# Converting the second network's weights in two of eight units, with partial results in the attention's PSUM banks

## The chip, the core and the metric

The kernel runs on one core of a Trainium2 chip. The metric is the device time of one launch in microseconds. The core has five engines with queues of their own: TensorE (PE) for matrix products, VectorE (DVE), ScalarE (ACT), GpSimd (POOL), and SyncE (SP), which issues the DMAs here. The engines wait for each other by semaphores. Each of them works its instructions off in the order in which the built program has them.

## The reference

Three stages follow each other: a gated linear attention over 768 time steps for 4 batches and 8 heads, a first network whose activation is a rational function, and a second one with a SoLU activation and a layer norm.

```python
for t in range(S):
    state = alpha[:, :, t, :, None] * state + np.einsum('bhd,bhe->bhde', k[:, :, t], v[:, :, t])
    y[:, :, t] = np.einsum('bhd,bhde->bhe', q[:, :, t], state)
...
h = x @ w_in
P = a[0] + a[1] * h + a[2] * h2 + a[3] * h3
Q = 1.0 + np.abs(b[0]) * np.abs(h) + np.abs(b[1]) * h2
g = P / (Q + 1e-06)
return (g @ w_out).astype(np.float32)
...
h = x @ w_in
sm = e / (np.sum(e, axis=-1, keepdims=True) + 1e-09)
solu = h * sm
ln = (solu - mu) / np.sqrt(var + 1e-06) * g_ln
return (ln @ w_out).astype(np.float32)
```

There are 3072 tokens of width 384; the first network is 2048 wide, the second 1024. The weights arrive as 64-bit floating-point numbers, so that they must be converted on the chip.

## The kernel before

The 768 steps are cut into 6 chunks of 128, and the first network works on one chunk (512 tokens over the batches) at a time, in 16 **units** of 128 columns of its hidden layer. So there are 96 units, numbered u from 0 to 95, in the loop at line 873. A unit multiplies up into a PSUM tile `hp` (line 590, 9 matmuls; every product is made of three, with values split into a high and a low part), evaluates the rational function on ACT, DVE and POOL (lines 595 to 624; on DVE the lines 616, 619, 620 and 621, and `fin[u]` is the last of them), and four units later multiplies down into `x2p` (line 636, 9 matmuls). `hp` has three PSUM banks, so the products of unit u + 3 wait for `fin[u]`.

The attention runs beside this, half a chunk in 8 units: six of the eight units have an attention step (`take(side, 1)`, line 900, begun anew where u modulo 8 is 2). The steps of PE are scores (`sc`, line 420), outputs (`y`, line 444) and state updates (`u`, line 483). All of them use one PSUM pool of two banks, the tag `at`. DVE reads `y` in line 471 and `u` in line 493. The steps of DVE prepare the next half chunk (lines 302 to 334: transposes, two scans, products).

The weights of the second network are converted in the same loop, by `w2_split`: 14 pieces, 6 of 128x512 and 8 of 128x384 numbers. A piece is loaded into a tile `st` (line 531), three integer operations on DVE put together a 32-bit number (lines 535, 538 and 539), ACT scales it (line 544, the last 8 pieces only) and makes the high part (545), POOL the low part (546), and a DMA writes both to DRAM (line 548). `st` has two buffers, which `x2e` (line 644, at the end of each chunk) uses too. The stage ends before u = 80, where the weights are read back.

Before the loop the weights of the first network go through the same `split_w`, with `stage["bank"]` at `"x2"`. There the result of lines 535 and 538, `fp`, lies in PSUM; from u = 0 on the bank is `""`, and `fp` is the SBUF tile `ft` itself.

The program is put in order by a scheduler that works from the order of the code and from dependencies. `later(n)` (line 839) adds one: what is issued in it stands behind `fin[u - n]`. `order` rows below show what comes of it.

Of the kernel before, what the change touches and what calls it, by code (L numbers as in the profile page):

```python
# [7 lines left out]
F32 = mybir.dt.float32  # L8
# [15 lines left out]
def _run(*gens):  # L24
    for g in gens:
        for _ in g:
            pass
# [3 lines left out]
def kernel(  # L31
# [23 lines left out]
    NTOK = B * CH  # L55
    KT = DM // 128
    NF1 = DF1 // 128
# [23 lines left out]
    SKIP = (5, 7, 11)  # L81
    AHEAD = 3
    LATE = 2
    U2, TP = 16, 0.3
    assert (B, H, D, CH) == (4, 8, 48, 128)

    const = ctx.enter_context(tc.tile_pool(name="const", bufs=1, side="left"))
# [55 lines left out]
    def judge(moe_pool):  # L143

        sums = const.tile([128, 1], F32, name="sums")
        row = moe_pool.tile([1, 128], F32, name="row", tag="ft", bufs=2)
        tot = const.tile([1, 1], F32, name="tot")
        nc.vector.tensor_reduce(sums, bad, axis=AX.X, op=ALU.add)
        nc.sync.dma_start(out=row, in_=sums)
        nc.vector.tensor_reduce(tot, row, axis=AX.X, op=ALU.add)  # L150
        nc.vector.tensor_scalar(flag, tot, 0.0, None, ALU.is_gt)

    def network(fast):
# [6 lines left out]
        ps_hp = ps_h.__enter__()  # L160
        if fast:
# [3 lines left out]
            ps_ap = ps_a.__enter__()  # L165
# [26 lines left out]
        def borrow(n, o, dims):  # L192
            if n not in lent:
                lent[n] = moe_pool.tile([128, GW], F32, name=f"lent{n}", tag=f"g{n}")
            size = 1
            for d in dims:
                size *= d
            t = lent[n][:, o:o + size]
            if len(dims) == 1:
                return t  # L200
            nm = "abcd"[:len(dims)]
            return t.rearrange(f"p ({' '.join(nm)}) -> p {' '.join(nm)}", **dict(zip(nm, dims)))
# [302 lines left out]
        stage = {"n": 0, "wide": False, "bank": None}  # L505

        def split_w(src, hi, lo, scale=None):
            keep = None
            if hi is None:
                keep, raw = lo, moe_pool.tile([128, NTOK], I64, name="st", tag="st", bufs=2)  # L510
                n = src.shape[1]
                both = raw[:].bitcast(F32R)
                hi, lo = both[:, :n], both[:, n:2 * n]
            n = src.shape[1]
            x = stage["n"]
            stage["n"] += 1
            ft = moe_pool.tile([128, NTOK], F32, name="ft", tag="ft", bufs=2)
            if stage["bank"] == "x2":
                fp = ps_x2p.tile([128, NTOK], F32, name="fp", tag=f"x2p{x % KT}")
            elif stage["bank"] == "h":  # L520
                fp = ps_hp.tile([128, NTOK], F32, name="fp", tag="h")
            else:
                fp = ft
            if src.dtype == I64:
                if keep is not None:
                    st = raw
                elif stage["wide"] and x % 6 not in (0, 2):
                    st = borrow(2, 2048 + 1024 * (0, 0, 0, 1, 2, 3)[x % 6], [2 * NTOK]).bitcast(I64)
                else:
                    st = moe_pool.tile([128, NTOK], I64, name="st", tag="st", bufs=2)  # L530
                nc.sync.dma_start(out=st[:, :n], in_=src)
                w32 = st[:, :n].bitcast(I32).rearrange("p (n t) -> p n t", t=2)
                fi = ft[:, :n].bitcast(I32)
                gi = fp[:, :n].bitcast(I32)
                nc.vector.tensor_scalar(  # L535
                    gi, w32[:, :, 1], 3, 0x3FFFFFF8, ALU.logical_shift_left, ALU.bitwise_and
                )
                nc.vector.scalar_tensor_tensor(gi, w32[:, :, 1], -0x40000000, gi, ALU.bitwise_and, ALU.bitwise_or)  # L538
                nc.vector.scalar_tensor_tensor(fi, w32[:, :, 0], 29, gi, ALU.logical_shift_right, ALU.bitwise_or)  # L539
            else:  # L540
                nc.sync.dma_start(out=ft[:, :n], in_=src)
            f = ft[:, :n]
            if scale is not None:
                nc.scalar.activation(f, f, AF.Copy, scale=scale)
            nc.scalar.activation(hi, f, AF.Copy)
            nc.gpsimd.tensor_tensor(lo, f, hi.bitcast(F32), ALU.subtract)
            if keep is not None:
                nc.sync.dma_start(out=keep, in_=both[:, :2 * n].bitcast(F32).rearrange("p (x n) -> p x n", x=2))
# [102 lines left out]
        def w2_split():  # L651
            nc.sync.dma_start(out=gln, in_=moe2_g_ln.rearrange("(f p) -> p f", p=128))
            for o in range(0, DF2, 512):
                for kt in range(KT):
                    split_w(moe2_w_in[128 * kt:128 * kt + 128, o:o + 512], None, w2i_d[:, :, kt, o:o + 512])
                    yield
            for f in range(NF2):
                split_w(moe2_w_out[128 * f:128 * f + 128, :], None, w2o_d[:, :, f, :], scale=gln[:, f:f + 1])
                yield

        def w2_load(nm):
            src = {"i": w2i_d, "o": w2o_d}[nm]
            n, step = {"i": (KT, 1), "o": (NF2, 4)}[nm]
            for z in range(0, n, step):
                for x, y in enumerate("hl"):
                    nc.sync.dma_start(out=w2[nm + y][:, z:z + step].bitcast(F32), in_=src[:, x, z:z + step])
                    yield
# [126 lines left out]
        def take(g, n):  # L794
            for _ in range(n):
                if next(g, "end") == "end":
                    return False
            return True

        def chain(*gens):  # L800
            for g in gens:
                yield from g
# [47 lines left out]
        def half_steps(i):  # L850
            gp = a_pe(i)
            gd = chain(a_prep(i + 1), a_move_qk(i + 1) if i + 1 >= NPE else iter(()), a_load(i + 2, ("ra", "rk")) if i + 2 < NH and i + 1 >= NPE else iter(())) if i + 1 < NH else iter(())
            while True:
                with pin(GP):
                    a = next(gp, "end")
                with pin(GS):
                    b = next(gd, "end")
                    if b != "end":
                        b = next(gd, "end")
                if a == "end" and b == "end":  # L860
                    if i + 1 < NH:
                        _run(a_enter(i + 1))
                        if i + 2 < NH and i + 1 < NPE:
                            _run(a_load(i + 2))
                    return
                yield

        split2 = w2_split() if fast else iter(())
        tp = 0.0
        side = iter(())  # L870
        tail = None
        prep = iter(())
        for u in range(NU + LAG):
            c, f = divmod(u, NF1)
            now[0] = u
            if f % (NF1 // 2) == LATE and u < NU:
                _run(side)
                i = 2 * c + 2 + f // (NF1 // 2)
                side = half_steps(i) if fast and i < NH else iter(())
            if u < NU:  # L880
                if f == 0 and c == NCH - 1:
                    if fast:
                        judge(moe_pool)
                    open2()
                    tail = chain(w2_load("i"), n_load(0), w2_load("o"))
                if f == 0 and c and not fast:
                    x_load(c)
                if fast and u < NF1:
                    if f % 4 == 0:
                        _run(prep)  # L890
                        prep = w1_group(f // 4 + 2) if f < 8 else iter(())
                    with later(G1):
                        take(prep, 1)
                m_up(u)
                if fast and u < NF1:
                    with later(G1):
                        take(prep, 1)
            if u == NU:
                _run(n_load(1))
            take(side, 1)  # L900
            if u >= U2:
                tp += TP
                with later(G2):
                    take(split2, int(tp))
                tp -= int(tp)
            if tail is not None:
                _run(split2)
                take(tail, 2)
            if u >= LAG:
                m_down(u - LAG)  # L910
            if u - NU + NF1 in EARLY:
                n_tile(EARLY.index(u - NU + NF1))
                if len(EARLY) == B and u - NU + NF1 == EARLY[-1]:
                    n_turn(0)
# [108 lines left out]
    with tc.If(wide > 0):  # L1023
        recurrence()
        network(False)
# [30 lines left out]
```

## Time and profile before

| | |
|---|---|
| median of 3 runs | 798.67 us (797.55 to 798.87) |
| the profiled execution | 796.42 us |
| its span, first to last instruction | 794.7 us |
| PE busy | 732.0 us, 92% of the span |
| DVE busy | 643.2 us, 81% |
| ACT busy | 535.5 us, 67% |
| POOL busy | 359.5 us, 45% |

The span is what the trace covers; 1.7 us of the execution's own time lie around it. Busy shares are means over stages. The unit loop runs to about 600 us of the span; what follows is the second network alone. A unit is recognized in the trace by its one ACT instruction of line 623, which makes the high part of its result.

### The profile page before, as it was taken

The page shows a single profiled execution, that of the slowest core. Times are in us where ns is not written, and L with a number is a line of the kernel's source. Part 1 is how long each engine was busy: PE and PEld are TensorE (multiplying, and loading weights), DVE is VectorE, ACT ScalarE, POOL GpSimd, SP SyncE. Part 2 cuts the span into 40 slices and gives each one's busy share as a digit, 9 for nine tenths or more (in the row PEclk, how much of TensorE's full clock was granted, in tenths as well). Part 3 has the DMA queues.
Part 4 walks back from the last instruction along what each step waited for, and adds up shares of the span by engine and source line. Part 5 has one row for each costly group of instructions (what it writes and reads, how often), then busy time and mean ns, then how long its engine had stood idle before and what let it go on. Part 6 is the DMA issues. An engine that isn't in the chain of part 4 may idle for free.

```text
span 794.7 us, 13903 instructions
## 1 busy us (share of the span) xinstructions
PE 732.0 (92%) x4976; PEld 606.9 (76%) x4976; DVE 643.2 (81%) x1110; ACT 535.5 (67%) x983; POOL 359.5 (45%) x306
## 2 busy tenths in 40 slices
PE   4864986999999989999999999999999999999996
PEld 3753765787777877687777788888888989998996
DVE  5999999979799998979897976567877698777630
ACT  2335756787787868788878879788775555455541
POOL 3256776856555344545454334243242524352322
PEclk9767898999999999999999999999999999999998
DMA  7956466365837275445826160460014443542552
GB/s 172 268 165 187 126 185 134 98 129 164 208 94 179 94 210 143 134 106 162 197 81 160 64 122 15 144 255 0 1 42 106 138 107 100 145 97 60 137 122 69
DMA packets 87279, 101.75 MB, mean 128 GB/s; under 512 B 34464, under 2 KB 63136, under 8 KB 87200
## 3 DMA queue, kind: packets, MB, share of 16 engines
q1 hardware_dynamic: 87104, 100.67, 48.0%
q8 instruction: 41, 0.67, 0.4%
q14 instruction: 38, 0.31, 0.1%
q10 hardware_dynamic: 96, 0.10, 0.0%
HBM read 60.59 MB, written 27.56 MB: 111 GB/s over the span
## 4 chain that ended last, share of the span: by engine, by line
PE 45%; DVE 27%; ACT 7%; DMA 7%; issue 7%; POOL 3%; SPq 3%; DVEq 0%; POOLq 0%; ACTq 0%
PE h L710 13%; PE op L774 12%; PE x2p L636 10%; PE hp L590 9%; DVE ft L539 2%; POOL gl L624 2%; SPq L266 2%; DVE p L616 2%; DVE w L619 2%; DVE alT L324 2%; DVE ft L538 2%; DVE qk L290 2%; DVE p L621 2%; DVE hp L620 2%; DVE ft L535 1%
## 5 line engine op out<-in xcount | busy, mean ns | idle before, releaser
L590 PE MATMUL hp<-xt,g 128*128 128x512 f32 x864 | 226.2, 404 | 16.7 <-DVE p L621 7.7
L590 PEld LDWEIGHTS hp<-xt,g 128*128 128x128 f32 x864 | 163.7, 193 | 59.5 <-DVE p L621 14.2
L624 POOL TENSOR_TENSOR gl<-p,gh 128x512 fp32r<-128x512 f32 x96 | 129.1, 1344 | 175.1 <-ACT gh L623 101.4
L636 PE MATMUL x2p<-gh,g 128*128 128x512 f32 x576 | 196.0, 395 | 0.6 <-ACT gh L623 0.6
L636 PEld LDWEIGHTS x2p<-gh,g 128*128 128x128 f32 x576 | 108.3, 189 | 26.3 <-ACT gh L623 1.4
L636 PE MATMUL x2p<-gl,g 128*128 128x512 f32 x288 | 113.6, 394 | 1.4 <-POOL gl L624 1.4
L774 PE MATMUL op<-w2oh,room 128*128 128x384 f32 x384 | 101.8, 339 | 0.1
L766 POOL TENSOR_TENSOR room<-room,room 128x1024 fp32r<-128x1024 f32 x22 | 53.6, 2438 | 102.2 <-ACT room L765 98.2
L619 DVE SCALAR_TENSOR_TENSOR w<-w,co,hp 128x512 f32<-128x512 f32 x84 | 61.8, 736 | 42.8 <-ACT hp L618 42.4
L710 PE MATMUL h<-w2ih,x 128*128 128x512 f32 x288 | 90.8, 394 | 0.0
L597 ACT ACTIVATE p<-hp,co 128x512 f32<-128x512 f32 x96 | 65.9, 687 | 13.9 <-POOL gl L624 13.4
L618 ACT ACTIVATE hp<-ah 128x512 f32<-128x512 f32 x84 | 50.1, 597 | 32.9 <-DVE p L616 32.2
L616 DVE SCALAR_TENSOR_TENSOR p<-p,co,hp 128x512 f32<-128x512 f32 x84 | 61.7, 734 | 12.7 <-ACT p L597 12.2
L598 ACT ACTIVATE w<-ah,co 128x512 f32<-128x512 f32 x96 | 69.3, 723 | 3.1 <-DVE hp L620 2.9
L774 PEld LDWEIGHTS op<-w2oh,room 128*128 128x128 f32 x384 | 70.0, 188 | 1.7 <-DVE room L766 0.5
L595 ACT ACTIVATE ah<-hp 128x512 f32<-128x512 f32 x96 | 56.7, 590 | 15.9 <-PE hp L590 15.8
L636 PEld LDWEIGHTS x2p<-gl,g 128*128 128x128 f32 x288 | 54.3, 189 | 14.5 <-POOL gl L624 2.6
L623 ACT ACTIVATE gh<-p 128x512 fp32r<-128x512 f32 x96 | 59.9, 624 | 8.1 <-PE x2p L636 3.0
L774 PE MATMUL op<-w2ol,room 128*128 128x384 f32 x192 | 65.0, 339 | 0.0
L621 DVE SCALAR_TENSOR_TENSOR p<-p,co,hp 128x512 f32<-128x512 f32 x84 | 62.2, 740 | 1.2
L710 PEld LDWEIGHTS h<-w2ih,x 128*128 128x128 f32 x288 | 53.9, 188 | 11.7
L617 ACT ACTIVATE ah<-w,co 128x512 f32<-128x512 f32 x84 | 60.6, 722 | 1.3
(168 smaller groups left out, 1281.1 us busy)
## 6 DMA issues: line engine op xcount, KB each, us to landing
room<-room SPq DMA_DIRECT2D x96, 128.0 KB, 2.3
qk_d<-qk SPq DMA_DIRECT2D x10, 771.0 KB, 4.0
st<-in_moe_w_in_dram SPq DMA_DIRECT2D x15, 512.0 KB, 4.9
st<-in_moe_w_out_dram SPq DMA_DIRECT2D x18, 384.0 KB, 4.2
qks<-qk_d SPq DMA_DIRECT2D x20, 257.0 KB, 5.1
x<-x_d SPq DMA_DIRECT2D x18, 256.0 KB, 3.7
out_dram<-o SPq DMA_DIRECT2D x94, 48.0 KB, 1.6
ra<-in_alpha_dram SPq DMA_DIRECT2D x44, 96.0 KB, 2.5
```

The costliest lines, as they stand in the source:

```text
L590: last["PE", u] = nc.tensor.matmul(hp, lhsT=w[:, kt, 128 * o:128 * o + 128], rhs=xts[c][:, kt, xx, :], start=(kt == 0 and w is hi and xx = ...
L597: nc.scalar.activation(p, hp, AF.Square, bias=co[:, 7:8])
L598: nc.scalar.activation(w, ah, AF.Square, bias=co[:, 6:7])
L616: nc.vector.scalar_tensor_tensor(p, p, a1, hp, ALU.add, ALU.mult)
L617: nc.scalar.activation(ah, w, AF.Ln, bias=rest)
L619: nc.vector.scalar_tensor_tensor(w, w, rest, hp, ALU.add, ALU.mult)
L621: fin[u] = nc.vector.scalar_tensor_tensor(p, p, a0, hp, ALU.add, ALU.mult)
L623: last["ACT", u] = nc.scalar.activation(gh, p, AF.Copy)
L624: last["POOL", u] = nc.gpsimd.tensor_tensor(gl, p, gh[:].bitcast(F32), ALU.subtract)
L636: nc.tensor.matmul(x2ps[c][d], lhsT=w[:, o, 128 * d:128 * d + 128], rhs=gg, start=(f == 0 and w is hi and gg is gh), stop=(f == NF1 - 1 an ...
L710: nc.tensor.matmul(hp[:, 512 * n:512 * n + 512], lhsT=x2s[c][:, kt, x, CH * b:CH * b + CH], rhs=w2[w][:, kt, 512 * n:512 * n + 512], start ...
L774: nc.tensor.matmul(op, lhsT=x[:, 128 * f:128 * f + 128], rhs=w2[w][:, f, :], start=(f == 0 and x is hi and w == "oh"), stop=(f == NF2 - 1 ...
```

## The change

A piece was converted whenever a running sum, which grew by 0.3 in each unit from u = 16 on, passed a whole number: about three pieces in ten units, whatever the attention did in that unit. Now a piece is converted in the units from u = 15 on whose number modulo 8 is 0 or 7, one in each: u = 15, 16, 23, 24, and so on to 64. The integer results `fp` go to a tile of the attention's PSUM pool. `later(G2)` is as before.

```diff
--- before.py
+++ after.py
@@ -81,7 +81,7 @@
     SKIP = (5, 7, 11)
     AHEAD = 3
     LATE = 2
-    U2, TP = 16, 0.3
+    U2, IDLE = NF1 - 1, (0, NF1 // 2 - 1)
     assert (B, H, D, CH) == (4, 8, 48, 128)
 
     const = ctx.enter_context(tc.tile_pool(name="const", bufs=1, side="left"))
@@ -517,8 +517,8 @@
             ft = moe_pool.tile([128, NTOK], F32, name="ft", tag="ft", bufs=2)
             if stage["bank"] == "x2":
                 fp = ps_x2p.tile([128, NTOK], F32, name="fp", tag=f"x2p{x % KT}")
-            elif stage["bank"] == "h":
-                fp = ps_hp.tile([128, NTOK], F32, name="fp", tag="h")
+            elif stage["bank"] == "at":
+                fp = ps_ap.tile([128, NTOK], F32, name="fp", tag="at")
             else:
                 fp = ft
             if src.dtype == I64:
@@ -866,7 +866,6 @@
                 yield
 
         split2 = w2_split() if fast else iter(())
-        tp = 0.0
         side = iter(())
         tail = None
         prep = iter(())
@@ -898,11 +897,10 @@
             if u == NU:
                 _run(n_load(1))
             take(side, 1)
-            if u >= U2:
-                tp += TP
+            if u >= U2 and f % (NF1 // 2) in IDLE:
+                stage["bank"] = "at"
                 with later(G2):
-                    take(split2, int(tp))
-                tp -= int(tp)
+                    take(split2, 1)
             if tail is not None:
                 _run(split2)
                 take(tail, 2)
```

On DVE the pieces now stand together. The rows are those of DVE in the second half of units 36 to 38, as they stand before: three pieces are near, two of them ahead of or between the two reads of `y` (L471).

```order
L535 TENSOR_SCALAR ft<-st 128x512
L619 SCALAR_TENSOR_TENSOR w<-w,co,hp 128x512
L538 SCALAR_TENSOR_TENSOR ft<-st,ft 128x512
L620 SCALAR_TENSOR_TENSOR hp<-w,hp 128x512
L539 SCALAR_TENSOR_TENSOR ft<-st,ft 128x512
L621 SCALAR_TENSOR_TENSOR p<-p,co,hp 128x512
L535 TENSOR_SCALAR ft<-st 128x384
L616 SCALAR_TENSOR_TENSOR p<-p,co,hp 128x512
L538 SCALAR_TENSOR_TENSOR ft<-st,ft 128x384
L471 TENSOR_TENSOR xt<-y,xt 128x2x256
L539 SCALAR_TENSOR_TENSOR ft<-st,ft 128x384
L471 TENSOR_TENSOR xt<-y,xt 128x256
```

After the change the same place, from the reads of `y` on:

```order
L471 TENSOR_TENSOR xt<-y,xt 128x2x256
L471 TENSOR_TENSOR xt<-y,xt 128x256
L620 SCALAR_TENSOR_TENSOR hp<-w,hp 128x512
L535 TENSOR_SCALAR fp<-st 128x384
L621 SCALAR_TENSOR_TENSOR p<-p,co,hp 128x512
L538 SCALAR_TENSOR_TENSOR fp<-st,fp 128x384
L539 SCALAR_TENSOR_TENSOR ft<-st,fp 128x384
L616 SCALAR_TENSOR_TENSOR p<-p,co,hp 128x512
L535 TENSOR_SCALAR fp<-st 128x384
L538 SCALAR_TENSOR_TENSOR fp<-st,fp 128x384
L539 SCALAR_TENSOR_TENSOR ft<-st,fp 128x384
L493 TENSOR_TENSOR Sbd<-Sbd,u 48x8x48 x2
```

The reads of `y` have moved ahead of the pieces, and two pieces stand as a block between them and L493, which frees the bank of `u`. It is so, with a row or two in between, for each pair of units.

On SP, the queue of the DMAs, the same half chunk begins with the store of the prepared `qk` and its reading back into `qks`, in the order before:

```order
L548 DMA w2i_d<-st 256x1x512
L276 DMA qks<-qk_d 32x4x514
L276 DMA qks<-qk_d 16x4x514 x2
L276 DMA qks<-qk_d 32x4x514
L548 DMA w2o_d<-st 256x1x384
L531 DMA st<-in_moe_w_out_dram 128x384
L348 DMA vns<-in_v_dram 128x8x48 x2
L282 DMA kns<-kb_d 128x4x192
L531 DMA st<-in_moe_w_out_dram 128x384
L548 DMA w2o_d<-st 256x1x384
L531 DMA st<-in_moe_w_out_dram 128x384
L266 DMA rq<-in_q_dram 32x4x192 x4
```

and after the change:

```order
L337 DMA qk_d<-qk 128x3x514
L276 DMA qks<-qk_d 32x4x514
L276 DMA qks<-qk_d 16x4x514 x2
L276 DMA qks<-qk_d 32x4x514
L348 DMA vns<-in_v_dram 128x8x48 x2
L282 DMA kns<-kb_d 128x4x192
L548 DMA w2o_d<-st 256x1x384 x2
L531 DMA st<-in_moe_w_out_dram 128x384 x2
L266 DMA rq<-in_q_dram 32x4x192 x4
```

The stores to `w2i_d` and `w2o_d` have moved behind the loads of `qks`, `vns` and `kns`, which the next half chunk of attention works on, and the loads of the next two pieces stand behind them as a pair.

## Rows read from the trace of the kernel before

**Rows 1.** Busy us of each engine by stretch, clock, DMA share, GB/s.
```profile
127.30:175.80 48.50, 43.48 (x320) 34.33 (x319) 42.61 (x67) 37.13 (x69) 34.27 (x31) 0.93 0.44 111
175.80:439.00 263.20, 248.81 (x1924) 198.47 (x1924) 237.46 (x376) 208.95 (x380) 129.64 (x116) 0.99 0.55 146
439.00:480.10 41.10, 40.62 (x323) 32.77 (x322) 34.64 (x58) 33.94 (x63) 15.15 (x14) 1.00 0.42 97
480.10:794.70 314.60, 307.35 (x1610) 267.89 (x1608) 212.22 (x385) 195.35 (x360) 110.93 (x70) 0.99 0.35 96
```

**Rows 2.** Timeline of ACT, line 623: start us, us, instruction.
```profile
175.78 0.62 ACT L623 ACTIVATE gh<-p 128x512 fp32r<-128x512 f32 x1
...
438.99 0.62 ACT L623 ACTIVATE gh<-p 128x512 fp32r<-128x512 f32 x1
...
480.06 0.62 ACT L623 ACTIVATE gh<-p 128x512 fp32r<-128x512 f32 x1
```

**Rows 3.** Waits of PE, 175.8 to 439.0: total us, times, longest.
```profile
PE hp L590 <- DVE p L621: 6.0, 7, 2.2
PE u L483 <- DVE xt L471: 5.9, 4, 1.9
PE y L444 <- POOL A L428: 2.0, 2, 1.9
```

**Rows 4.** Two short stretches, columns as in rows 1.
```profile
199.40:202.80 3.40, 3.10 (x7) 2.48 (x8) 3.40 (x6) 1.58 (x3) 0.78 (x1) 0.50 1.00 303
240.30:243.80 3.50, 3.50 (x74) 3.32 (x64) 3.50 (x8) 1.66 (x3) 1.45 (x3) 0.51 0.36 139
```

**Rows 5.** Groups by line and shape, DVE, 175.8 to 439.0, conversions alone.
```profile
L539 DVE SCALAR_TENSOR_TENSOR ft<-st,ft 128x384 int32<-128x384 int32 x8 | 6.4, 803 | 0.1
L535 DVE TENSOR_SCALAR ft<-st 128x384 int32<-128x384 int32 x8 | 5.8, 720 | 0.8 <-DMA st<-in_moe_w_out_dram 0.8
L539 DVE SCALAR_TENSOR_TENSOR ft<-st,ft 128x512 int32<-128x512 int32 x6 | 5.7, 958 | 0.0
L538 DVE SCALAR_TENSOR_TENSOR ft<-st,ft 128x384 int32<-128x384 int32 x8 | 5.5, 689 | 0.1
L538 DVE SCALAR_TENSOR_TENSOR ft<-st,ft 128x512 int32<-128x512 int32 x6 | 5.1, 854 | 0.1
L535 DVE TENSOR_SCALAR ft<-st 128x512 int32<-128x512 int32 x6 | 4.5, 746 | 1.7 <-DMA st<-in_moe_w_in_dram 1.7
```

**Rows 6.** Timeline of DVE, POOL and PE about 292 us.
```profile
292.25 1.27 POOL L624 TENSOR_TENSOR gl<-p,gh 128x512 fp32r<-128x512 f32 x1 [0.85 <-ACT gh L623]
292.34 1.59 DVE L539 SCALAR_TENSOR_TENSOR ft<-st,ft 128x384 int32<-128x384 int32 x1
...
292.47 1.14 PE L483 MATMUL u<-vns,kns 128*64 128x48 f32 x32 [1.92 <-DVE xt L471]
```

**Rows 7.** Lines 535, 538, 539: ns min/median/max, starts, shapes.
```profile
L535 DVE TENSOR_SCALAR ft<-st x28: 344/518/1650, 66.0 to 417.9; 128x384 int32<-128x384 int32 x16, 128x512 int32<-128x512 int32 x12
...
L535 DVE TENSOR_SCALAR fp<-lent x9: 545/548/739, 17.7 to 60.9; 128x384 int32<-128x384 int32 x6, 128x512 int32<-128x512 int32 x3
...
L538 DVE SCALAR_TENSOR_TENSOR fp<-lent,fp x9: 545/550/687, 20.7 to 62.7; 128x384 int32<-128x384 int32 x6, 128x512 int32<-128x512 int32 x3
...
L539 DVE SCALAR_TENSOR_TENSOR ft<-lent,fp x9: 525/537/674, 23.5 to 65.1; 128x384 int32<-128x384 int32 x6, 128x512 int32<-128x512 int32 x3
```

**Rows 8.** Waits of DVE, 439.0 to 480.1.
```profile
DVE w L619 <- ACT hp L618: 4.4, 4, 1.6
```

**Rows 9.** Timeline of DVE and PE, 471 to 475 us.
```profile
471.37 0.75 DVE L621 SCALAR_TENSOR_TENSOR p<-p,co,hp 128x512 f32<-128x512 f32 x1
...
474.38 2.20 PE L590 MATMUL hp<-xt,g 128*128 128x512 f32 x9
```

**Rows 10.** DMA issues, 175.8 to 439.0: KB each, median us to landing.
```profile
w2i_d<-st SPq DMA_DIRECT2D x6, 512.0 KB, 3.4
st<-in_moe_w_out_dram SPq DMA_DIRECT2D x8, 384.0 KB, 4.6
```

## Prediction

> **What bounds the kernel now.** I read the busy time by stretch first. The unit loop's conversions fall between the ACT instruction of line 623 of u = 15 (175.8 us) and that of u = 63 (439.0): 48 units, six cycles of eight [rows 2]. These take 263.2 us, 43.9 a cycle. The cycle after them, u = 63 to 71, has the same attention steps, but for the state update of lines 493 and 494 (two short operations of DVE and two of POOL), and no conversion, and takes 41.1 [rows 1, 2]. There PE is busy for 40.6 of 41.1 us: it is bound by PE. In the six cycles PE is busy for 248.8 of 263.2, so 14.4 us are idle. After 480.1 us PE is busy for 307 of 314.6 us [rows 1], and nothing of that stage is changed; what the loop gains or loses should pass to the end one for one.
>
> Next, the waits of PE in the six cycles: 6.0 us for line 621 (a rational function that comes late, so that no `hp` bank is free), 5.9 us for line 471 (the read of `y`, which frees the bank that `u` needs), and 2.0 us for POOL's mask of line 428 [rows 3]. All three name engines that also convert. A fourth cost hangs on the stalls: in two stretches, together 6.9 us, the granted clock is half, the 1.2 of the two levels 1.2 and 2.4 GHz [rows 4]. The first follows PE's wait of 2.2 us for line 621. At half the rate they lose about 3.4 us of work.
>
> Last, the conversions themselves. The 14 pieces take 33.0 us of DVE in these cycles (the sum of six groups), 720 to 958 ns an operation [rows 5]. A single operation is far from that mean: line 535 runs from 344 to 1650 ns [rows 7]. At 292.3 us the reader sees a long one. Line 539 takes 1.59 us beside a POOL instruction of 1.27 us which began just ahead of it; it stands between the two reads of `y` in DVE's order, and PE's line 483 has waited 1.92 us for them when it begins [rows 6].
>
> **What the change removes.** If conversions were wholly free, each of the six cycles would take 41.1 us: 263.2 - 6 x 41.1 = 16.6 us less. From PE's side it is 13.9 us of waits and 3.4 us of half clock, less the 0.5 us that PE idles in a clean cycle too, six times: 14.3 us. I take 15.5, the middle. Bounds: 14.3 and 16.6.
>
> **What PSUM does to the operations.** The first network's conversions, before the loop, already have `fp` in PSUM. Of those from `lent` tiles, 27 operations, none is longer than 0.74 us; the minima are 545, 545 and 525 ns (the 384-wide ones), the maxima 739, 687 and 674 (512) [rows 7]. So a piece costs 1.6 to 2.1 us in the new form, and 14 pieces 8 x 1.6 + 6 x 2.1 = 25.4 us instead of 33.0. POOL ran beside them in that stage, though with other instructions; so I take the 25.4 as holding. The 7.6 us are part of the 15.5 us, not to be added.
>
> One thing speaks against PSUM: the shortest line 535 is 344 ns in SBUF and 545 in PSUM [rows 7], so that without collisions the change would make DVE's work longer, by at least 14 x 0.2 = 2.8 us. The Trainium skill states this in VectorE: DVE Perf Modes, Why PSUM operands drop a tier: an operand in PSUM shuts out the mode that uses both SBUF read ports, and fp32 falls to the single rate. The trace agrees with the two minima. By that rule alone the sum below would be 2.8 us smaller if DVE's time counted one for one, 9.2 us; by the rows it is not, since the long operations outweigh it.
>
> **What the change adds.** A pair of pieces now stands in each cycle, from u = 15 on, seven pairs, 3.2 us each (384) or 4.2 (512). By the order, the block stands behind the reads of `y`, between line 616 and line 619 or close to it. Its cover is this: in the clean cycle DVE waits four times in the units after the attention's preparation for line 618 of ACT, 4.4 us in total, at most 1.6 [rows 8]. PE sets the pace there, and DVE has 41.1 - 34.6 = 6.5 us free in the whole cycle [rows 1]. The pair uses the wait of its own unit, about 1.4 us (between the mean of 1.1 and the 1.6). It then delays line 621 of this unit by 3.2 - 1.4 = 1.8 us, or 4.2 - 1.4 = 2.8. PE's margin there: line 621 of u = 70 ends at 472.1, and the matmuls of u = 73, which need its bank, begin at 474.4, so 2.3 us [rows 9]. A 384 pair is hidden, a 512 pair costs PE 0.5. The rest of the slip shrinks by some 1.1 us in each of the next two units; what is left, 0 to 0.6 us, delays the attention's next preparation. So a cycle gives back 0 to 1.1 us. I take 0.5, six times 3.0 us. If the cover were gone, a pair would cost its 3.2 or 4.2 us.
>
> The first pair (u = 15, 16) comes in a cycle that had none of these pieces. DVE is unbusy there for 48.5 - 42.6 = 5.9 us [rows 1], against 4.2: from 0 to 2 us, I take 0.5. ACT and POOL do the same operations as before, earlier or later by a few units. ACT waits in order for line 539, with units behind it in its queue; this is in the same slip.
>
> The PSUM banks: both tiles of a pair use the bank of the second `y` tile, which is read by then, so nothing waits to begin; the scores of the next half chunk come two units of PE (over 8 us) after the block. I take 0. The DMAs are the same in number. On SP the stores of a pair, 3.4 us, now come behind the loads for the next attention step instead of among them, and the loads, 4.6 us, stand behind the stores [rows 10]; they are needed some 30 us later. I take 0 here too, and the late load as a rival.
>
> **Sum.** 15.5 - 3.0 - 0.5 = 12.0 us. The profiled execution of 796.4 (span 794.7) becomes 784.4. The median of the runs shown lies 2.3 us above that execution, at 798.67, so I forecast 786.7. With the bounds, 14.3 - 6.6 - 2 = 5.7 and 16.6 - 0 - 0 = 16.6, the forecast case reaches from 782 to 793.
>
> **Rivals.**
> - **DVE's quantity counts, not the place** (0.22). DVE is busy for 237.5 of the 263.2 us in the six cycles [rows 1]. If every microsecond of it counted, only the shorter operations would show: 7.6 us less, 791.1. The row on line 471 speaks against it [rows 3, 6]: an operation hurts PE where it stands.
> - **Nothing changes** (0.07). PE's idle time would come from the attention's preparation, which stands in the same units before and after, and the pairs would bring as much slip as they take away. The clean cycle, with this preparation and 0.5 us of PE idle, speaks against it. 798.7.
> - **Late loads** (0.10), slower. Both loads of a pair wait on SP for stores of the pair before, or for `x2e`, which has the same two buffers. A block of two pieces waits at the head of DVE's queue, and with it lines 493, 619 and 621, and the scores whose banks the pair holds. Once before, line 535 waited 1.7 us for its load [rows 5]. Store and load after each other are 8 us [rows 10]. Beyond the margin of 2.3 and the 12.0 / 7 = 1.7 us of gain per pair, so from 4 us of lateness on, the kernel is slower; at 5 us it would be 7 x 5 - 7 x 4, 7 us above before: 805.7.
> - **The PSUM tier alone** (0.03), slower. If POOL stretches the operations in PSUM just as it did in SBUF, and every microsecond of DVE counts, the 2.8 us come on top: 801.5. The 27 operations speak against it [rows 7]. This is what the Trainium skill's rule on PSUM operands (VectorE: DVE Perf Modes) would make of it.
>
> **How the numbers follow.** The forecast has the rest, 0.58. About 0.2%, 1.6 us, is what a measurement of this kernel can tell from no change. Faster is the forecast and the quantity rival, 0.80; same is 0.07; slower 0.13. The range from 780.5 to 796.5 holds nearly all of the first two cases; it leaves out the others and a little at both ends, 2 in 10.
>
> **What the profile after would show.** Right: the 14 first operations with `fp<-st` in the loop all under 0.75 us, and about 25 us in total for lines 535, 538 and 539; PE's waits for lines 471 and 621 from 13.9 (with line 428) down to 3 to 5 us; six cycles of about 41.6; no half clock in the loop after u = 15; DVE's wait for line 618 halved, because the pairs fill it. Wrong: cycles of 43 us with PE waiting for line 621 two or three units after a pair (the slip is not absorbed); DVE waiting in front of line 535 for a DMA (late loads); operations with `fp` of over 1 us (PSUM doesn't keep POOL out).

## The result, and the profile after

The changed kernel takes 785.77 us (median of 4 runs, 783.2 to 786.84) against 798.57 for the kernel before beside it. The ratio is 0.9833, with a 95% interval of 0.981 to 0.9855: 1.7% faster. The forecast was 786.7. The profiled execution took 786.76 us, with a span of 784.9.

The busy time by stretch, cut at the same instructions of line 623 as [rows 1] (u = 7, 15, 63 and 71), with the same columns:

```profile
128.50:178.80 50.30, 44.71 (x325) 35.02 (x324) 46.53 (x73) 37.18 (x70) 36.33 (x33) 0.93 0.52 137
178.80:429.10 250.30, 244.94 (x1937) 196.29 (x1936) 228.25 (x372) 208.37 (x379) 126.54 (x115) 1.00 0.57 147
429.10:469.30 40.20, 39.23 (x308) 31.18 (x304) 34.23 (x56) 33.29 (x61) 15.13 (x14) 1.00 0.41 99
469.30:784.90 315.60, 307.63 (x1611) 268.10 (x1609) 214.11 (x385) 195.14 (x360) 111.94 (x70) 0.99 0.35 96
```

The six cycles take 250.3 us where they took 263.2. PE's idle time in them fell from 14.4 to 250.3 - 244.9 = 5.4 us. Its busy time fell too, by 3.9 us. The granted clock is 1.00 in the whole stretch: the two half-clock stretches of [rows 4], in which PE was busy for 6.6 us, are gone, and half of that, 3.3 us, is most of the 3.9. The cycle from u = 7 to 15, which has the first pair now, took 1.8 us longer; the one from 63 to 71 took 0.9 us less. A single cycle cut at line 623 is not a good measure, though: the cut moves against PE's work with ACT's order, and the changed kernel has 308 matmuls between its last two cuts where the kernel before had 323. Together, from u = 7 to 71, 352.8 us became 340.9: 11.9 us less. Of these its span shows 9.8 (794.7 to 784.9), since this part of it began 1.2 us later and the work behind it took 0.9 us longer, in code that the change does not touch.

The waits of PE in the six cycles, columns as in [rows 3]:

```profile
PE u L483 <- DVE xt L471: 2.5, 4, 1.0
PE x2p L636 <- ACT x2e L644: 1.4, 4, 0.5
PE y L444 <- POOL A L428: 0.9, 2, 0.5
PE hp L590 <- DVE p L621: 0.4, 2, 0.2
```

13.9 us became 5.2. The wait for line 621 has nearly gone, 6.0 to 0.4, and no wait is longer than 1.0 us. The conversions by line and shape, as in [rows 5], for all 14 pieces (160 to 429 us):

```profile
L538 DVE SCALAR_TENSOR_TENSOR fp<-st,fp 128x384 int32<-128x384 int32 x8 | 4.5, 559 | 0.2
L535 DVE TENSOR_SCALAR fp<-st 128x384 int32<-128x384 int32 x8 | 4.5, 558 | 0.2
L539 DVE SCALAR_TENSOR_TENSOR ft<-st,fp 128x384 int32<-128x384 int32 x8 | 4.4, 552 | 0.2
L535 DVE TENSOR_SCALAR fp<-st 128x512 int32<-128x512 int32 x6 | 4.1, 691 | 0.5 <-DMA st<-in_moe_w_in_dram 0.4
L538 DVE SCALAR_TENSOR_TENSOR fp<-st,fp 128x512 int32<-128x512 int32 x6 | 4.1, 690 | 0.1
L539 DVE SCALAR_TENSOR_TENSOR ft<-st,fp 128x512 int32<-128x512 int32 x6 | 4.1, 682 | 0.1
```

They take 25.7 us where they took 33.0. The minimum, median and maximum of line 538 over the whole kernel, to be held against [rows 7], tell the two memories apart in one execution:

```profile
L538 DVE SCALAR_TENSOR_TENSOR fp<-st,fp x19: 527/597/696, 13.2 to 415.4; 128x384 int32<-128x384 int32 x10, 128x512 int32<-128x512 int32 x9
L538 DVE SCALAR_TENSOR_TENSOR ft<-st,ft x14: 523/825/2134, 67.8 to 140.1; 128x384 int32<-128x384 int32 x8, 128x512 int32<-128x512 int32 x6
```

With the partial result in PSUM the longest of 19 took 0.70 us; with both inputs in SBUF, in the units before the change begins to act, 14 took from 0.52 to 2.13. (The neighbours on POOL are not the same for the two groups.) The timeline of one pair, at 245 us, with POOL and PE beside it (start, duration, instruction), answers to [rows 6]:

```profile
244.25 1.01 DVE L471 TENSOR_TENSOR xt<-y,xt 128x512 fp32r<-128x512 f32 x2
244.99 1.14 PE L483 MATMUL u<-vns,kns 128*64 128x48 f32 x32 [0.99 <-DVE xt L471]
245.30 0.69 DVE L535 TENSOR_SCALAR fp<-st 128x512 int32<-128x512 int32 x1
...
248.19 1.30 POOL L546 TENSOR_TENSOR st<-ft,st 128x512 fp32r<-128x512 f32 x1 [3.43 <-ACT st L545]
248.74 0.69 DVE L538 SCALAR_TENSOR_TENSOR fp<-st,fp 128x512 int32<-128x512 int32 x1
249.46 1.29 POOL L624 TENSOR_TENSOR gl<-p,gh 128x512 fp32r<-128x512 f32 x1
249.46 0.69 DVE L539 SCALAR_TENSOR_TENSOR ft<-st,fp 128x512 int32<-128x512 int32 x1
```

Both reads of `y` are done before the first piece begins, so PE's line 483 has waited 0.99 us, not 1.92. And line 539 begins with POOL's line 624, as it did in [rows 6], and takes 0.69 us where it took 1.59. The Trainium skill has a rule for this in GPSIMD Engine Reference, Specifications: GpSimd's SBUF interface is shared with VectorE and contends with instructions that have two SBUF inputs or run in a mode with two ports. The trace agrees for the two inputs: 1.59 us with both in SBUF, 0.69 us with one in PSUM.

### The profile page after: what moved, and what is told of

Its sections match the earlier page's. It is cut to its first block, busy times and chain, and to the rows that moved or that the text cites. A ratio compares the mean times of both kernels' runs of the same rounds, so it can differ in the third digit from the quotient of the medians.

```text
span 784.9 us, 13904 instructions
## 1 busy us (share of the span) xinstructions
PE 730.2 (93%) x4976; PEld 605.3 (77%) x4976; DVE 639.8 (82%) x1110; ACT 534.5 (68%) x983; POOL 359.9 (46%) x306
## 3 DMA queue, kind: packets, MB, share of 16 engines
q1 hardware_dynamic: 87104, 100.67, 48.5%
## 4 chain that ended last, share of the span: by engine, by line
DVE 28%; PE 17%; ACT 13%; issue 5%; SPq 4%; DMA 4%; POOL 1%; ACTq 0%; DVEq 0%; POOLq 0%
PE x2p L636 6%; PE hp L590 6%; DVE room L750 3%; SPq L760 3%; DVE room L733 2%; PE op L774 2%; ACT jk L735 2%; DVE p L616 2%; DVE hp L620 2%; DVE w L619 2%; DVE sm L729 2%; DMA room<-room 2%; DMA rq<-in_q_dram 2%; DVE room L748 2%; PE h L710 2%
## 5 line engine op out<-in xcount | busy, mean ns | idle before, releaser
L595 ACT ACTIVATE ah<-hp 128x512 f32<-128x512 f32 x96 | 56.5, 589 | 13.7 <-PE hp L590 13.6
```

## The experiments

All are compared with the kernel before on the same chip, whose median was 797.8 to 799.1 us there, so that the ratios tell more than the medians. A gain "by the ratios" is the ratio's distance from 1, taken of this median. The last two columns are from each profiled execution: the time from line 623 of u = 7 to that of u = 71 (from the starts of these two instructions), and the time of the conversions on DVE.

| kernel | median us | ratio, 95% interval | u = 7 to 71 | conversions |
|---|---|---|---|---|
| before | 798.57 | 1 | 352.8 | 33.0 |
| the change | 785.77 | 0.9833 (0.981 to 0.9855) | 340.9 | 25.7 |
| 1 place alone | 795.74 | 0.9978 (0.9961 to 0.9995) | 351.0 | 32.2 |
| 2 PSUM alone | 789.59 | 0.9887 (0.9869 to 0.9904) | 344.9 | 25.8 |
| 3 units with attention preparation | 804.14 | 1.0074 (1.0058 to 1.0091) | 358.0 | 34.3 |
| 4 place behind `y`, SBUF | 791.21 | 0.9906 (0.9886 to 0.9926) | 346.1 | 27.1 |
| 5 the same, last pair in PSUM | 789.99 | 0.988 (0.986 to 0.9899) | 342.8 | 26.3 |
| 6 line 538 twice | 787.02 | 0.985 (0.983 to 0.987) | 342.4 | 34.4 |
| 7 line 538 left out | 787.64 | 0.9851 (0.9832 to 0.987) | 342.8 | 17.2 |
| 8 no conversion on DVE | 793.76 | 0.9944 (0.993 to 0.9959) | 348.3 | 0 |
| 9 first pair moved on | 786.23 | 0.9847 (0.9827 to 0.9866) | 343.4 | 25.8 |
| 10 last six pieces late, one by one | 788.11 | 0.9857 (0.9833 to 0.988) | 342.4 | 25.8 |

### 1 and 2: each half of the change alone

The first leaves the new units and takes the bank away, so `fp` is in SBUF; the second takes the kernel before and only sets the bank.

```diff
 # 1, from the changed kernel
             if u >= U2 and f % (NF1 // 2) in IDLE:
-                stage["bank"] = "at"
                 with later(G2):
 # 2, from the kernel before
                 tp += TP
+                stage["bank"] = "at"
                 with later(G2):
```

> The conversions in the two units of eight as after the change, but with the partial results in SBUF as before. In the built order the first piece of most pairs then stands ahead of the reads of y (line 471), because no bank holds it back. Theory (what counts is what a piece delays, and long operations beside POOL): lines 535, 538 and 539 take about 33 us in the loop again instead of 25, PE waits for line 471 for about 1 us a cycle, and the time is 789 to 794 us. Rival (only the quantity of DVE work counts, not the place): as before the change, 797 to 800 us.

> The conversions at the old rate of 0.3 a unit from u = 16, but with the partial results in the attention's PSUM banks. Theory: no operation of lines 535, 538 and 539 over 0.75 us, 25 us in total, but pieces remain ahead of the attention's preparation; 789 to 794 us, with PE waits for line 621 of 3 us or more. Rival (quantity alone): 7.6 us less than before, 791 us, the same as the whole change within its own error, so that the place would add nothing.

The place alone is worth little, 0.2%, between the two expectations. PSUM alone is worth 1.1%. Its time is where the theory had it and also near the rival's 791, but the rival wanted it equal to the whole change, and the two intervals are apart. Two signs of the theory were off a little: the longest conversion took 0.79 us, and PE waited 2.4 us for line 621, not 3. The gains of the two, 1.8 and 9.0 us by their ratios, come to 10.8 of the change's 13.3; within the intervals the difference of 2.5 is not shown. Kernel 1 still has long conversions, 32.2 us, and this wait of PE in its six cycles:

```profile
PE u L483 <- DVE xt L471: 6.5, 5, 1.5
```

Its order tells why: the first piece of each pair (of the first two pairs, its line 535 alone) stands ahead of the reads of `y`, as in the kernel before. One such place (timeline of DVE and PE):

```profile
285.34 1.83 DVE L535 TENSOR_SCALAR ft<-st 128x384 int32<-128x384 int32 x1
...
289.46 1.01 DVE L471 TENSOR_TENSOR xt<-y,xt 128x512 fp32r<-128x512 f32 x2
...
290.20 1.14 PE L483 MATMUL u<-vns,kns 128*64 128x48 f32 x32 [1.45 <-DVE xt L471]
```

In the changed kernel the piece's tile is in the bank of `y`, and so it has to come behind them. Thus the bank does two things: it makes the operations short, and it sets their place within the unit. Kernel 2 has both effects, since many of its pieces stand behind the reads of `y` too; how much of its 9.0 us belongs to either, it does not tell. In kernel 2 the bank sets the place badly once. A piece holds the bank while its own operations stand apart on DVE, and PE's next `y` waits for line 539; the granted clock is half just behind that wait (timeline, then busy time by stretch):

```profile
199.36 0.43 PE L444 MATMUL y<-qks,Sbd 128*32 128x128 f32 x8 [3.21 <-DVE ft L539]
```

```profile
200.50:203.90 3.40, 3.40 (x31) 2.60 (x21) 0.27 (x1) 0.40 (x2) 0.82 (x1) 0.50 0.69 249
```

### 3: the units with the attention's preparation

```diff
-    U2, IDLE = NF1 - 1, (0, NF1 // 2 - 1)
+    U2, IDLE = NF1 - 1, (4, 5)
...
-                stage["bank"] = "at"
```

> One piece in each of the units whose number modulo 8 is 4 or 5, partial results in SBUF: by the built order the pieces stand just ahead of and inside the attention's preparation on DVE. Compared with the run that has them in 0 and 7 with SBUF, only the place differs. Theory (place): the pieces cost nearly their whole 33 us, 803 to 812 us, PE waits for line 621 of over 12 us. Rival (quantity): as before the change, 797 to 800 us.

The time is the theory's, and against kernel 1, with SBUF in both, it prices the choice of units at 8.4 us. The theory's sign is not there: PE waits 4.2 us for line 621, not 12. PE's waits are spread over four releasers, 15.3 us in all, and the half clock comes on top. (Line 614 ends the rational function in the even units below 24, where 621 does elsewhere.) The waits of PE in its six cycles, and one of its half-clock stretches:

```profile
PE hp L590 <- DVE p L621: 4.2, 3, 1.7
PE y L444 <- POOL A L428: 3.8, 3, 1.4
PE u L483 <- DVE xt L471: 3.7, 2, 1.9
PE hp L590 <- DVE p L614: 3.6, 1, 3.6
```

```profile
294.90:301.70 6.80, 6.03 (x42) 5.07 (x43) 5.88 (x10) 4.77 (x9) 3.37 (x3) 0.50 0.91 194
```

### 4 and 5: the place within the unit, without PSUM

Both hold the pieces behind the second read of `y` (line 471) by a rule of the scheduler, with `fp` in SBUF. The second does so for the first six pairs and leaves the last one in PSUM.

```diff
 # 4
-                stage["bank"] = "at"
-                with later(G2):
+                read = max((k for k in marks if k[1:] == (1,)), default=None)
+                with later(G2), tc.issue_after(marks[read].ins) if fast else ExitStack():
 # 5, besides
+                stage["bank"] = "at" if u >= NU - 33 else ""
+                hold = fast and not stage["bank"]
+                with later(G2), tc.issue_after(marks[read].ins) if hold else ExitStack():
```

> The changed kernel with the partial results in SBUF, and each piece made to stand behind the second read of y (line 471) by an order of its own, which the PSUM banks gave before. So the places are those of the changed kernel, and only the memory of fp differs. Theory A (long operations beside POOL are the larger half): about 31 to 33 us for the three lines, 790 to 794 us. Theory B (the order behind the reads of y was what the banks gave): 785 to 788 us, near the changed kernel.

> The changed kernel with the partial results of the first six pairs in SBUF, these pieces held behind the second read of y by a rule of their own; the last pair has its bank in PSUM, as in the change. Theory A (what the bank in PSUM gives is the place behind the reads of y, and the loss of the version in SBUF with that rule, 791.2, came from its last pair alone): 785 to 788 us, with cycles of 42 us up to u = 63 and the cycle from 63 to 71 back at 40 to 41. Rival B (the memory itself is worth some us, through operations that POOL's work doesn't stretch): 789 to 792 us, with the loss in the cycles up to u = 63.

Kernel 4 took the time that theory A gave, 0.9906: the hold alone turns the 0.2% of kernel 1 into 0.9%. But theory A's reason did not come. It wanted 31 to 33 us of conversions, and they took 27.1, against 32.2 in kernel 1 and 25.7 in the change: in this place the operations are nearly short without PSUM too. The loss against the change lies in part in one cycle, u = 63 to 71, which took 45.0 us with a wait of 2.0 us for line 621 and a half clock behind it:

```profile
430.20:475.10 44.90, 42.32 (x321) 34.09 (x320) 36.59 (x59) 35.74 (x66) 17.48 (x14) 0.96 0.39 97
455.20:458.60 3.40, 3.40 (x9) 2.66 (x9) 3.33 (x6) 1.20 (x3) 1.28 (x1) 0.50 0.56 210
```

Nor is the place quite that of the change: in kernels 4 and 5 the second piece of the last pair stands behind line 493 and begins some 7 us later than in the change, at 421.9 and 421.5 us against 414.8.

Kernel 5 was to tell whether that cycle was all. It was not: without that half clock the stretch from u = 7 to 71 comes to 342.8 us, 1.9 above the change, and the median is 789.99, rival B's value. By line 623 the last cycle takes 43.2 us, but that is the cut again, with 328 matmuls against 308. Cut at PE's own state updates (line 483), where the matmuls agree, the time up to the last pair and the last pair's cycle are, in the change and then in kernel 5:

```profile
161.40:412.00 250.60, 244.99 (x1926) 196.46 (x1925) 228.26 (x370) 207.86 (x377) 129.87 (x118) 1.00 0.58 150
412.00:454.70 42.70, 41.63 (x322) 32.74 (x322) 38.06 (x65) 35.47 (x65) 18.04 (x18) 1.00 0.44 112
```

```profile
161.80:414.30 252.50, 245.80 (x1925) 195.59 (x1924) 226.01 (x369) 206.14 (x374) 130.42 (x118) 1.00 0.58 149
414.30:457.30 43.00, 42.32 (x323) 33.75 (x322) 38.73 (x66) 37.08 (x68) 19.71 (x18) 1.00 0.46 115
```

So the loss in the trace, 1.9 us and then 0.3, lies where B expected it (kernel 4 has 253.2 and 45.2 us, 2.6 and then 2.5 more). B's reason, stretched operations, is seen in the first two pairs above all (two of 1.13 and 1.28 us at 207 to 211 us), but it is small in sum: 26.3 us of conversions against 25.7.

With the place nearly given, the memory itself is worth between 1.9 us (by the traces) and 3.7 us (by the two ratios, 0.47%); the intervals of the two ratios just miss each other. By what means stays open. (The profiled execution of kernel 5, at 793.35 us the slowest of its four, lost another 4.3 us behind u = 71, in code that is the same.)

### 6 and 7: DVE's quantity

Line 538 issued twice, or not at all, in the pieces of the loop: 8.5 us more or less work for DVE in the same place. The edit is that of kernel 6; kernel 7 puts the line itself under `if keep is None`.

```diff
                 nc.vector.scalar_tensor_tensor(gi, w32[:, :, 1], -0x40000000, gi, ALU.bitwise_and, ALU.bitwise_or)
+                if keep is not None:
+                    nc.vector.scalar_tensor_tensor(gi, w32[:, :, 1], -0x40000000, gi, ALU.bitwise_and, ALU.bitwise_or)
```

> The changed kernel with line 538 done twice in each of the 14 pieces (the second time changes no bit), 8.5 us of DVE work more, 1.2 us for each pair. Theory (a pair stands in time that DVE has free, but that time is nearly used up: 2.5 to 4.3 us a cycle are left): 787 to 791 us, less than half of the added work shows to all of it being hidden but for 1 us. Rival (DVE's quantity counts one for one): 794 us.

> The changed kernel, with line 538 left out in the 14 pieces of the loop (so the second network's weights are not the real ones): 8.5 us less work for DVE. Theory (the pairs lie in DVE's free time behind the reads of y, and PE sets the pace): almost nothing of it is gained, 784 to 786 us, with cycles of 41 to 42 us. Rival (DVE's quantity counts one for one): 777 to 778 us.

Over 17 us of DVE work the median moves by 1.9 us at most, and in no order: 787.64 without line 538, 785.77 with it, 787.02 with two of them. The three ratios lie within 0.2% and their intervals overlap. Kernel 6 came where the theory had it. Kernel 7 is 1.6 us slower than the theory's range, away from the rival's 777. The six cycles of kernel 6 and of kernel 7, busy times as above:

```profile
180.20:432.20 252.00, 245.20 (x1937) 196.17 (x1938) 234.42 (x383) 208.01 (x380) 127.65 (x115) 1.00 0.57 146
```

```profile
180.30:432.00 251.70, 245.18 (x1927) 195.42 (x1928) 221.47 (x358) 206.69 (x378) 125.73 (x115) 1.00 0.55 146
```

DVE is not busy for 252.0 - 234.4 = 17.6 us in kernel 6, 22.1 in the changed kernel, 30.2 in kernel 7. What is taken from DVE there comes back as its own waits; kernel 7's, and the changed kernel's beside them (line 619 stands on line 620 in kernel 7):

```profile
DVE w L620 <- ACT hp L619: 19.4, 23, 1.8
DVE p L617 <- ACT p L598: 5.2, 12, 0.9
```

```profile
DVE w L619 <- ACT hp L618: 14.2, 18, 1.1
DVE p L616 <- ACT p L597: 3.1, 8, 0.9
```

The 12 pieces in these cycles lost 8 x 0.56 + 4 x 0.69 = 7.2 us of work, and the two waits grew by 5.2 + 2.1 = 7.3. In this place the conversions are covered, in both directions, to within the 1 to 2 us that these runs can tell. In kernel 6 the cover runs short: PE waits again for the last line of the rational function, 621 in the change (0.4 us there), 623 here:

```profile
PE hp L592 <- DVE p L623: 3.2, 5, 1.2
```

### 8: no conversion on DVE at all

The three DVE operations are left out, and ACT's scaling reads the high words instead (the weights are not the real ones).

```diff
+                if keep is None:
                     ...
-            if scale is not None:
-                nc.scalar.activation(f, f, AF.Copy, scale=scale)
+            if keep is not None:
+                nc.scalar.activation(f, w32[:, :, 1].bitcast(F32), AF.Copy, scale=1.0 if scale is None else scale)
```

> As after the change, but the three DVE operations of a piece are left out: ACT takes the high words of the 64-bit numbers as they are (6 pieces have one ACT operation more), so the second network's weights are not the real ones. Loads, stores, ACT and POOL work stay. Theory (a pair is nearly hidden in the time that DVE has free): 780 to 784 us, 2 to 6 us under the changed kernel, though 25 us of DVE work are gone. Rival (quantity): the loop falls to PE's floor of about 40.2 us a cycle, 774 to 777 us.

Both were wrong: 793.76 us, about 8 more than with the conversions. The waits of ACT name the cause (line 544 stands on 545):

```profile
ACT ft L545 <- DMA st<-in_moe_w_out_dram: 11.7, 5, 4.3
ACT ft L545 <- DMA st<-in_moe_w_in_dram: 7.4, 3, 4.3
```

With no DVE operation ahead of it, and no bank to hold it, ACT's first operation of a piece stands earlier in ACT's order than its load lands, and 19.1 us of ACT are spent waiting, with the units' lines 595 to 618 behind it; the changed kernel has no such wait in these cycles. PE's own waits come to 10.8 us there, where the change has 5.2, and 6.8 us at half clock follow. Leaving work out took its place away too, so this kernel says nothing on the quantity; kernels 6 and 7 were made for that.

### 9 and 10: where the pairs go

Kernel 9 begins with the second pair's units (u = 23), kernel 10 gives a list of units that leaves the cycles from u = 48 to 68 free and converts the rest in single pieces from u = 69 on.

```diff
 # 9
-    U2, IDLE = NF1 - 1, (0, NF1 // 2 - 1)
+    U2, IDLE = NF1 + 7, (0, NF1 // 2 - 1)
 # 10
+    WHEN = (23, 24, 31, 32, 39, 40, 47, 48, 69, 71, 73, 75, 77, 79)
...
-            if u >= U2 and f % (NF1 // 2) in IDLE:
+            if u in WHEN:
```

> The changed kernel with the pairs from u = 23 on instead of 15, so that the last pair stands in u = 71 and 72. The cycle from u = 7 to 15, which took 50.3 us with the first pair and 48.5 without, should be back at 48.5, and the one from u = 63 to 71 should take about 1 us more. Theory: 784 to 786 us, a gain of about 1 us. Rival (the 1.8 us of that cycle were chance): no change or 1 us slower.

> The changed kernel with pieces in u = 23, 24, 31, 32, 39, 40, 47, 48 and then one in every second unit from 69 to 79, where no half chunk of attention is prepared any more and DVE has 15 us free in eight units. Theory (a pair still costs 1 to 2 us in a cycle with attention, and nothing there): 780 to 783 us. Rival (a piece every second unit waits for its load, since two buffers take load, work and store in turn): 787 us or more, with DVE waiting in front of line 535.

Kernel 9 came where its rival had the time: nothing was gained. By line 623 its cycle from u = 7 to 15 has its 48.5 us back and the one from 63 to 71 takes 42.4 where the change has 40.2, but much of that is the cut. By line 483 the cycle of the first pair takes 42.5 us without the pair and 42.3 with it, and the one that has the pair at the end takes 41.3 against 40.3. Kernel 10's two cycles without a pair are, cut at line 483,

```profile
369.40:410.40 41.00, 40.06 (x320) 32.62 (x320) 36.57 (x59) 32.67 (x60) 19.52 (x17) 1.00 0.47 110
410.40:450.90 40.50, 40.47 (x322) 33.05 (x322) 35.38 (x59) 34.28 (x61) 16.77 (x16) 1.00 0.47 117
```

where the same two take 41.5 and 42.7 us in the change. So a pair does cost its cycle something, 0.5 and 2.2 us here. But the rest came as its rival had it. A load that comes late stops DVE, and the bank that the piece holds passes this on to PE (timeline):

```profile
463.68 1.27 SPq L531 DMA_DIRECT2D st<-in_moe_w_out_dram  x2
...
466.69 0.56 DVE L535 TENSOR_SCALAR fp<-st 128x384 int32<-128x384 int32 x1 [3.88 <-DMA st<-in_moe_w_out_dram]
...
468.41 0.55 DVE L539 SCALAR_TENSOR_TENSOR ft<-st,fp 128x384 int32<-128x384 int32 x1
...
469.01 1.28 PE L420 MATMUL sc<-qks 48*128 48x128 f32 x6 [2.27 <-DVE ft L539]
```

```profile
469.40:476.30 6.90, 6.90 (x20) 5.48 (x20) 5.58 (x9) 6.78 (x13) 2.89 (x3) 0.51 0.17 59
```

One late load cost DVE 3.9 us, the scores 2.3, and then 6.9 us at half clock: the cycle took 46.5 us.

## Why the prediction was right, and where it was off

**The sum.** From u = 7 to 71 the forecast was 12.0 us less, and 11.9 came. That this agrees to a tenth is in part luck, as its terms show when the cycles are cut at line 483. The kernel before has there

```profile
160.20:424.40 264.20, 249.81 (x1930) 199.31 (x1929) 237.49 (x376) 210.54 (x381) 132.22 (x119) 0.99 0.55 147
424.40:465.40 41.00, 40.56 (x321) 32.74 (x321) 34.85 (x59) 33.86 (x62) 16.78 (x16) 1.00 0.34 91
```

and the change 250.6 and 42.7 us (shown with kernel 5). The last cycle, which now has a pair, takes 1.7 us more, where a pair was put at 0.5 and at most 1.1. Five cycles can be compared with and without a pair: 1.7 here and 2.2 for the same cycle by kernel 10, 0.5 (kernel 10 too), 1.0 and -0.2 (kernel 9). Their mean is about 1.0, an estimate from single executions; so seven pairs cost nearer 7 us than the 3.5 of the sum, and what the change removed is then nearer 19 than 15.5, above its upper bound of 16.6. By this estimate two terms were too small, and they cancel. By PE's idle time a pair is nearer the forecast: 5.4 us in the six cycles, 0.9 each, against 0.5 in the clean cycle before. Which measure is the better one stays open.

The forecast of the median, 786.7 for 785.77, has luck in it too. The profiled execution was put at 784.4 and took 786.76: 2.1 us of the gain are missing at its two ends for no reason of the change. But its median lies 1.0 us below it, where the forecast had added 2.3.

**What the conversions cost in PSUM** was right: 25.7 us against 25.4, none of the 42 operations above 0.75 us. Reading it from the first network's conversions in the same trace [rows 7] was a sound way. The rule that PSUM operands drop a tier (the Trainium skill, VectorE: DVE Perf Modes, Why PSUM operands drop a tier) holds for line 535 here too: its shortest in the loop was 0.35 us with SBUF in kernels 4 and 5, and 0.55 in the changed kernel. It decided nothing, since those 0.2 us are of DVE's quantity, and kernels 6 and 7 show that its quantity is covered there.

**The place, not the quantity** was right as a mechanism, and kernel 3 against kernel 1 prices it at 8.4 us. But the prediction read the place as the choice of units, and treated the bank only as a matter of duration and of waits that it might add. The order of the change, with the pieces behind the reads of `y`, came from the bank (in the first two pairs not all of it is one block ahead of line 493, though): without it, the new units alone give 1.8 us (kernel 1), and with a hold in its stead they give 7.5 (kernel 4; both by their ratios). That PSUM's part would be the larger one was not foreseen.

**The cover** of the pairs was right in kind: a pair, and even a pair with a third more work, is mostly taken up by DVE's waits. Two of its signs were off. PE's waits came to 5.2 us, a little over the 3 to 5 that were given, 1.4 of it for line 644 at the ends of the chunks, which did not show before. And DVE's wait for line 618 did not halve. It was 13.7 us in the kernel before,

```profile
DVE w L619 <- ACT hp L618: 13.7, 14, 1.6
```

and is 14.2 now. The base of this sign was wrong: the 4.4 us of [rows 8] are those of a clean cycle, six of which make 26.4, and the kernel before, with its conversions, had only half of that to begin with.

**The rivals.** DVE's quantity is refuted by kernels 6 and 7. Late loads did not come in the changed kernel, where the waits for `st` in the six cycles are 0.4 us; the mechanism is real, and kernel 10 shows it with 3.9 us. No change, and the PSUM tier alone, are refuted by the result. No wait of PE in the six cycles, before or after, names a DMA; what the moved stores and loads on SP do by themselves was not tested.

## What to carry to other kernels

Ask of work on a busy but not limiting engine where it stands between the instructions that the limiting engine waits for, before counting how long it takes: here 8.5 us more or less of DVE work changed nothing that could be told from the spread of the runs, while the choice of units and the place behind the reads of `y` were worth 8 and 6 us (kernels 3 and 4 against kernel 1). A buffer is also an order: putting a result into a bank that another step must free moves the work behind that step, for good here and for bad in kernel 2. To test such a change, add or drop work in the same place; leaving it all out takes away what held the order.

## What was not expected of the hardware

A short wait of PE can cost more than its own length, if the half clock that comes behind it is its doing. In these traces a half granted clock follows a wait of 3.2 us (kernel 2), of 2.0 (kernel 4), and of 2.3 (kernel 10), for 3.4, 3.4 and 6.9 us; the changed kernel, with no wait over 1.0 us in the six cycles, has none there. Both stretches of [rows 4] are of this kind: the first follows the wait of 2.2 us for line 621, and the second, at 240.3 us, follows the longest wait for POOL's mask in [rows 3]:

```profile
239.35 0.41 PE L444 MATMUL y<-A,vns 128*32 128x128 f32 x4 [1.87 <-POOL A L428]
```

But the wait of 1.92 us at 292 us [rows 6] has no half clock behind it. What sets the two apart the traces do not show.
